# Moving one pattern matmul of each head pair and spreading the finishing of two batches over four pairs, in an attention and mixture-of-experts kernel on one Trainium2 core

## The chip, the core and the metric

The kernel runs on one core of one Trainium2 chip. The metric is the device time of one execution in microseconds (us). The engines are named as in the profile: PE is TensorE (matmuls and transposes; PEld its weight loads), DVE is VectorE, ACT is ScalarE, POOL is GpSimd, SP is SyncE. L305 is line 305 of the kernel before.

## The reference, cut to what matters

Four batches, eight heads, 768 tokens, head size 64. Every query and key falls into one of 64 buckets by the signs of six projections, and a query sees the keys of its own bucket only. The attention's result is then routed token by token to one of eight experts.

```python
q_bits = (einsum('bhsd,dk->bhsk', q, proj) > 0)      # keys likewise
mask = q_bucket[:, :, :, None] == k_bucket[:, :, None, :]
scores = where(mask, q @ k.T / 8, -1e9)
attn = softmax(scores) @ v                           # (4, 8, 768, 64)
x = attn.transpose(0, 2, 1, 3).reshape(3072, 512)
logits = x @ w_gate + modality_bias[modality_id]     # (3072, 8)
e_idx = argmax(logits); gate_w = softmax(logits)[e_idx]
out = gate_w * (relu(x @ w1[e_idx]) @ w2[e_idx])     # w1 512x1024, w2 1024x512
```

## The kernel before

Heads are worked on in 16 pairs, four pairs to a batch: pair `i` belongs to batch `i // 4`. One turn of the outer loop over `i` computes the scores of pair `i`, and prepares later pairs beside it: row maxima (`maxp`) of pair `i + 1`, transposes, signs and patterns (`turn`, `signs`, `patterns`) of pair `i + 2`, and the splitting of the loads (`split`) of pair `i + 3`. Each of these is a Python generator that yields after each piece of work.

The order of PE's instructions is written by hand (`manual_schedule`). Each turn has six strings, `PLAN[0]` to `PLAN[5]`, called string 0 to string 5 here, and each letter takes one piece from one generator. The order of the instructions on the other engines is made by a scheduler, which keeps the data's dependencies and starts what is ready; it lets an instruction that first writes a tile wait until the tile that had the buffer before has been read for the last time.

The letters that matter here:
- `S` one of three score pieces of a string (L305, L306), whose result ACT puts through the exponential (L318, L323); `A` the weighing of the values (L341).
- `M` a row-maximum piece: a matmul (L239 or L245), whose result DVE reduces (L241, L247). `B` is `maxp_back`: PE transposes the negated maxima (L268), and DVE reads the result with three instructions (L270, L270, L271).
- `T` the next of the transposes (L180), signs (L207, read by DVE L209) and patterns (L222, read by L223 and L224) of pair `i + 2`. These are twelve pieces; the strings hold eleven `T`, and `P` takes the twelfth, the last pattern of the second head, in the next turn's string 0.
- `Q` is `sums(i - 1)`: eight matmuls (L359) whose result DVE copies into a new tile `gs` (L362, first pair of a batch) or adds to it (L364).
- `F`, `f`, `E`, `e` take one piece of `finish(b)`, in the four pairs after batch `b`. Its 19 pieces in order: 1 and 2 matmuls for the logits (L374); 3 and 4 their six transposes (L383), read by DVE L384; 5 three transposes of the batch's `gs` (L390), read by L391; 6 L400; 7 L402 to L404; 8 L408; 9 L411; 10 to 13 the routing (`route`: L591 to L597, L600 to L604, small matmuls L609 and L611 with L614 to L617, L620 to L628); 14 to 19 six scatters by POOL into a table in memory (L631).
- `x`, `y` take the pieces of `finish_x` (transposes L422), which writes a batch's attention result to memory, in the third and fourth pair.

Everything that PE writes outside the scores, the maxima and the weighing goes through one pool of two PSUM buffers, `ps_x` (tile `psx`): `T`, `P`, `B`, `Q`, the vector sums `V`, the finishing's matmuls and transposes, and `x`. The maxima have two buffers of their own (`psm`), the scores two (`pss`). The tile `gs` is in a pool with one buffer:

```python
bp = ctx.enter_context(tc.tile_pool(name="bp", bufs=1))
...
        if c == 0:
            gsum[b] = bp.tile([P, HALF], F32, name="gs")
...
        gs = gsum[b]     # in finish(b), piece 5
```

After the 16 pairs the expert stage runs, from about 535 us on; the change does not touch it.

Of the kernel before, what the change touches and what calls it, by code (L numbers as in the profile page):

```python
# [27 lines left out]

LAG = 2
PLAN = (  # L30
    "LvSPMTMSASfMTMfexy",
    "SMTVMSASfMTMey",
    "SMTMSAQFlSMTMEfxy",
    "SMSATWSBMEe",
    "SWMSATFSMTMfWExe",
    "SMTSATSBFfFfWe",
)
FIRST = "mtmtmtmtmtmtmtmbmssnTnbssTnTnTnTnTnTnbTnTTTbT"


# [29 lines left out]
def chain(*gens):  # L70
    for g in gens:
        yield from g


def attention(ctx, actx, tc, a, x_d, l_d, route=None, setup=None):
    nc = tc.nc
    q, k, v, proj = a["q"], a["k"], a["v"], a["proj"]
    NPR = a.get("npair", NP)
# [75 lines left out]
    def split(i, heads=(0, 1)):  # L154

        t = st[i]
        t["n2"] = t.get("n2", {})
        for h in heads:
            qk = t["qk"][h]
            n = nat.tile([P, 2, NT, P], F32R, name="n2")  # L160
            (nc.vector.tensor_copy if i == 0 and h in CFG['rv'] else nc.scalar.copy)(out=n[:, 0, :, 0:64], in_=qk[:, 0])
            nc.scalar.copy(out=n[:, 1, :, 64:128], in_=qk[:, 1])  # L162
            yield
            for x in range(2):
                e = (CFG["rs"] if i == 0 else "PPPP" if i in CFG["rq"] else CFG["sub"])[2 * h + x]
                (nc.vector if e == "D" else nc.gpsimd).tensor_tensor(  # L166
                    out=n[:, x, :, 64 - 64 * x:128 - 64 * x], in0=qk[:, x], in1=n[:, x, :, 64 * x:64 + 64 * x].bitcast(F32), op=ALU.subtract)
            t["n2"][h] = n
            yield

    def turn(i, heads=(0, 1)):

        t = st[i]
        t.update(gens[(i + 2) % 3])
        for h in heads:
            for g in range(3):
                tp = ps_x.tile([P, MAIN], F32, name="psx")
                for j in range(4):
                    x, tt = divmod(4 * g + j, NT)
                    nc.tensor.transpose(tp.bitcast(F32R)[:, j * P:(j + 1) * P], t["n2"][h][:, x, tt], identr)  # L180
                for x in range(2):
                    lo, hi = max(4 * g, NT * x), min(4 * g + 4, NT * x + NT)
                    if lo < hi:
                        (nc.vector.tensor_copy if i == 0 and g == 1 and h in CFG['rv'] else nc.scalar.copy)(
                            out=(t["m2"], t["s2"])[x][h][:, (lo - NT * x) * P:(hi - NT * x) * P], in_=tp[:, (lo - 4 * g) * P:(hi - 4 * g) * P])
                if i == 0 and h == 0:
                    if g == 1:
                        nc.vector.tensor_copy(out=t["m1"][h][QK[h]], in_=t["m2"][h][0:64].bitcast(F32))
                    if g == 2:
                        nc.vector.tensor_copy(out=t["s1"][h][QK[h]], in_=t["s2"][h][64:128].bitcast(F32))  # L190
                else:
                    if g == 1:
                        nc.sync.dma_start(out=t["m1"][h][QK[h]].bitcast(F32), in_=t["m2"][h][0:64].bitcast(F32))
                    if g == 2:
                        nc.sync.dma_start(out=t["s1"][h][QK[h]].bitcast(F32), in_=t["s2"][h][64:128].bitcast(F32))
                yield

    def signs(i, heads=(0, 1)):

        t = st[i]  # L200
        bt = bits[(i + heads[0]) % 2]
        rows = slice(64 * heads[0], 64 * heads[-1] + 64)
        for half in range(2):
            hs = slice(half * HALF, (half + 1) * HALF)
            z = ps_x.tile([P, MAIN], F32, name="psx")
            for o in range(2 * heads[0], 2 * heads[-1] + 2):
                nc.tensor.matmul(z[32 * o:32 * o + 32, 0:HALF], zst, (t["m2"], t["s2"])[o % 2][o // 2][:, hs].bitcast(F32),  # L207
                                 start=True, stop=True, tile_position=(0, 32 * o))
            nc.vector.tensor_scalar(out=bt[rows, hs], in0=z[rows, 0:HALF], scalar1=0.0, scalar2=0.5, op0=ALU.is_gt, op1=ALU.subtract)  # L209
            yield  # L210

    def patterns(i, heads=(0, 1), before=()):

        for _ in before:
            yield
        t = st[i]
        bt = bits[(i + heads[0]) % 2]
        for half in range(2):
            hs = slice(half * HALF, (half + 1) * HALF)
            for h in heads:  # L220
                pp = ps_x.tile([P, MAIN], F32, name="psx")
                nc.tensor.matmul(pp[:, 0:HALF], pat[:, h], bt[:, hs], start=True, stop=True)  # L222
                (nc.vector.tensor_copy if (half if i > 1 else i + h == 0) else nc.scalar.copy)(out=t["m1"][h][PT[h], hs], in_=pp[0:64, 0:HALF])  # L223
                nc.scalar.activation(t["s1"][h][PT[h], hs], pp[64:128, 0:HALF], AF.Relu)  # L224
                yield
# [203 lines left out]
    def first():  # L429

        late = []
        for g in (split(0, (0,)), turn(0, (0,)), split(0, (1,)), signs(0, (0,)), patterns(0, (0,))):
            for _ in g:
                pass
        g = {"m": maxp(0, late, (0,)), "t": chain(turn(0, (1,)), signs(0, (1,)), patterns(0, (1,))),
             "n": maxp(0, late, (1,)), "s": split(1), "T": chain(turn(1), signs(1), patterns(1))}
        for c in FIRST:
            if c == "b":
# [6 lines left out]
    with tc.manual_schedule(engines={mybir.EngineType.PE}):  # L445
        load(1)
        load_v(0)
        load(2)
        first()
        wg = sm.tile([P, 4, 8], F32, name="wg", bufs=1)  # L450
        nc.sync.dma_start(out=wg, in_=a["moe_w_gate"].rearrange("(c p) e -> p c e", p=P))
        gst = fconst.tile([P, 4, 32], F32, name="gst")
        nc.gpsimd.memset(gst, 0.0)
        nc.gpsimd.tensor_copy(out=gst[0:64, :, 0:8], in_=wg[0:64])
        nc.gpsimd.tensor_copy(out=gst[64:128, :, 16:24], in_=wg[64:128])
        ones = fconst.tile([P, 4, 32], F32, name="ones")
        nc.gpsimd.memset(ones, 0.0)
        for c in range(4):
            nc.gpsimd.memset(ones[:, c, c:c + 1], 1.0)
        if setup is not None:  # L460
            setup()
        avs = weigh()
        fins = xs = ts = iter(())
        for i in range(NPR):
            late = []
            ss = score(i)
            ms = maxp(i + 1, late) if i + 1 < NPR else iter(())
            last, ts = ts, chain(turn(i + 2), signs(i + 2), patterns(i + 2)) if i + 2 < NPR else iter(())
            ws = split(i + 3) if i + 3 < NPR else iter(())
            if i % 4 == 0 and i > 0:  # L470
                fins = finish(i // 4 - 1)
            for kt in range(NT):
                for c in PLAN[kt]:
                    if c == "S":
                        next(ss)
                    elif c == "M":
                        next(ms, None)
                    elif c == "T":
                        next(ts, None)
                    elif c == "P":  # L480
                        next(last, None)
                    elif c == "W":
                        next(ws, None)
                    elif c == "A":
                        if i > 0 or kt >= LAG:
                            next(avs)
                    elif c == "B":
                        if late:
                            late.pop(0)()
                    elif c == "v":  # L490
                        vadds(i)
                    elif c == "V":
                        vsums(i)
                    elif c == "Q":
                        if i > 0:
                            sums(i - 1)
                    elif c == "L":
                        if i + 3 < NPR:
                            load(i + 3)
                    elif c == "l":  # L500
                        if i + 1 < NPR:
                            load_v(i + 1)
                    elif c == "F" and i % 4 == 0 or c == "f" and i % 4 == 1:
                        next(fins, None)
                    elif c == "e" and i % 4 >= 2 or c == "E" and i == NPR - 2:
                        next(fins, None)
                    elif c == "x" and i % 4 == 2 or c == "y" and i % 4 == 3:
                        if c == "x" and kt == 0 and i > 4:
                            xs = finish_x(i // 4 - 1, 0, NT)
                        next(xs, None)  # L510
                        next(xs, None)
        for _ in avs:
            pass
        sums(NPR - 1)
# [4 lines left out]
E = 8  # L519
# [463 lines left out]
```

## Time and profile before

| what | value |
|---|---|
| median of three executions | 880.5 us (880.32, 880.5, 881.27) |
| the profiled execution's own time | 876.6 us |
| its span, first to last instruction | 874.7 us |
| PE busy | 815.4 us, 93% |
| DVE, ACT, POOL busy | 584.8, 506.2, 457.1 us |
| mean granted TensorE clock | 0.985 |
| start of pair 1, of pair 15 | 62.7 us, 507.7 us |

A group of instructions in the profile is one line, engine and operation. "Idle before" is the time an engine did nothing before an instruction; the name behind the arrow is what ended that wait. A pair's turn is measured from its first score matmul to the next pair's.

### The profile page before, as it was taken

The page shows a single profiled execution, that of the slowest core. Times are in us where ns is not written, and L with a number is a line of the kernel's source. Part 1 is how long each engine was busy: PE and PEld are TensorE (multiplying, and loading weights), DVE is VectorE, ACT ScalarE, POOL GpSimd, SP SyncE. Part 2 cuts the span into 40 slices and gives each one's busy share as a digit, 9 for nine tenths or more (in the row PEclk, how much of TensorE's full clock was granted, in tenths as well). Part 3 has the DMA queues.
Part 4 walks back from the last instruction along what each step waited for, and adds up shares of the span by engine and source line. Part 5 has one row for each costly group of instructions (what it writes and reads, how often), then busy time and mean ns, then how long its engine had stood idle before and what let it go on. Part 6 is the DMA issues. An engine that isn't in the chain of part 4 may idle for free.

```text
span 874.7 us, 14543 instructions
## 1 busy us (share of the span) xinstructions
PE 815.4 (93%) x5154; PEld 579.8 (66%) x5154; DVE 584.8 (67%) x1029; ACT 506.2 (58%) x953; POOL 457.1 (52%) x347
## 2 busy tenths in 40 slices
PE   5899999998999998999998898879999999999993
PEld 3555655654665554665554555779999999998993
DVE  7776676678677678667776876955555555667550
ACT  5666766665666565566664364444555555557551
POOL 5387678757688757687756687322222221123010
PEclk9899999999999999999999999999999999999997
DMA  6423212221332321340210163796777776677750
GB/s 178 115 60 91 64 41 77 74 54 55 98 85 72 91 60 32 97 118 22 55 46 9 31 229 120 166 266 196 230 231 218 222 227 215 209 240 267 229 155 22
DMA packets 76753, 110.87 MB, mean 127 GB/s; under 512 B 10495, under 2 KB 52095, under 8 KB 76672
## 3 DMA queue, kind: packets, MB, share of 16 engines
q1 hardware_dynamic: 70880, 95.14, 37.6%
q0 software_dynamic: 4928, 13.14, 4.0%
q10 hardware_dynamic: 864, 1.57, 0.9%
q8 instruction: 43, 0.70, 0.4%
q14 instruction: 38, 0.31, 0.1%
HBM read 84.83 MB, written 13.33 MB: 112 GB/s over the span
## 4 chain that ended last, share of the span: by engine, by line
PE 77%; DVE 10%; ACT 4%; DMA 3%; issue 3%; POOL 2%; SPq 0%; POOLq 0%; ACTq 0%; DVEq 0%
PE psu L341 14%; PE pss L305 8%; PE pss L306 6%; PE psm L239 5%; PE yps L835 5%; PE yps L837 5%; PE yps L836 5%; PE hps L795 4%; PE hps L794 4%; PE hps L793 4%; PE psx L207 3%; PE psx L180 3%; PE psm L245 3%; PE psx L222 2%; DVE mx L241 1%
## 5 line engine op out<-in xcount | busy, mean ns | idle before, releaser
L326 POOL TENSOR_TENSOR sp<-sp,pb 128x768 f32<-128x768 f32 x124 | 225.3, 1841 | 42.0 <-ACT pb L323 40.6
L758 DVE TENSOR_TENSOR w<-raw,w 128x1024 fp32r<-128x1024 f32 x108 | 134.9, 1250 | 94.4 <-ACT w L756 93.3
L756 ACT CAST w<-raw 128x1024 fp32r<-128x1024 f32 x112 | 117.2, 1047 | 63.2 <-PE yps L837 55.9
L341 PE MATMUL psu<-pb,vt 128*64 128x512 f32 (+1 forms) x768 | 147.0, 505 | 0.0
L241 DVE TENSOR_REDUCE mx<-psm 128x1 f32<-128x512 f32 x192 | 127.6, 685 | 23.1 <-PE psm L239 22.4
L318 ACT ACTIVATE pb<-pss 128x512 f32<-128x512 f32 x192 | 114.9, 599 | 42.3 <-PE pss L306 22.8
L323 ACT ACTIVATE pb<-pss 128x512 f32<-128x512 f32 x96 | 57.5, 599 | 125.7 <-PE pss L306 122.8
L793 PE MATMUL hps<-xh,w 128*128 128x256 f32 x384 | 108.9, 284 | 2.4 <-DVE hl L800 2.4
L794 PE MATMUL hps<-xl,w 128*128 128x256 f32 x384 | 108.9, 284 | 0.0
L795 PE MATMUL hps<-xh,w 128*128 128x256 f32 x384 | 108.5, 283 | 0.0
L341 PEld LDWEIGHTS psu<-pb,vt 128*64 128x64 f32 x768 | 47.2, 137 | 88.4 <-issue 88.2
L770 POOL DMA_INDIRECT xg<-x_d,tb x26 | 30.8, 1184 | 125.9 <-DMA tb<-tab 87.7
L843 POOL DMA_INDIRECT out<-y,tb x26 | 34.0, 1309 | 118.0 <-ACT y L842 61.3
L835 PE MATMUL yps<-w,hl 128*128 128x512 f32 x208 | 83.6, 402 | 1.9 <-DVE hl L823 1.9
L837 PE MATMUL yps<-w,hh 128*128 128x512 f32 x208 | 81.8, 393 | 0.0
L836 PE MATMUL yps<-w,hh 128*128 128x512 f32 x208 | 81.7, 393 | 0.0
L247 DVE TENSOR_REDUCE mx<-psm 128x2 f32<-128x512 f32 x96 | 66.1, 689 | 22.7 <-PE psm L245 21.5
L305 PE MATMUL pss<-m_0g,s_0g 128*128 128x512 f32 x192 | 78.2, 407 | 0.0
L793 PEld LDWEIGHTS hps<-xh,w 128*128 128x128 f32 x384 | 73.4, 192 | 3.7 <-DVE hl L800 3.0
L166 POOL TENSOR_TENSOR n<-qk,n 128x384 fp32r<-128x384 f32 x36 | 39.7, 1109 | 67.3 <-ACT n L162 60.0
L794 PEld LDWEIGHTS hps<-xl,w 128*128 128x128 f32 x384 | 73.6, 192 | 1.7 <-issue 1.2
L795 PEld LDWEIGHTS hps<-xh,w 128*128 128x128 f32 x384 | 73.5, 192 | 0.0
(214 smaller groups left out, 1763.0 us busy)
## 6 DMA issues: line engine op xcount, KB each, us to landing
raw<-moe_w SPq DMA_DIRECT2D x112, 512.0 KB
qk<-q SPq DMA_DIRECT2D x32, 192.0 KB
qk<-k SPq DMA_DIRECT2D x32, 192.0 KB
vt<-v SPq DMA_DIRECT2D x16, 384.0 KB
x_d<-xs SPq DMA_DIRECT2D x18, 256.0 KB
m_1g<-m_1g SPq DMA_DIRECT2D x16, 192.0 KB
s_1g<-s_1g SPq DMA_DIRECT2D x16, 192.0 KB
m_0g<-m_0g SPq DMA_DIRECT2D x15, 192.0 KB
```

What stands on the lines that cost most here:

```text
L241: nc.vector.tensor_reduce(out=mx[:, qt + j, hi, 0:1], in_=mp, axis=AX.X, op=ALU.max)
L305: nc.tensor.matmul(out, t["s1"][h][:, ks], t["m1"][h][:, cs], start=True, stop=False)
L326: (nc.vector if h and i in CFG["spd"] else nc.gpsimd).tensor_tensor(out=t["sp"][:, h], in0=(t["pb"][0] if kt == 1 else t["sp"])[:, h], in1 ...
L341: nc.tensor.matmul(t["u"][part][64 * h:64 * h + 64, 0:w], t["v"][:, h, kt], t["pb"][kt][:, h, COLS[part]], start=False, stop=(kt == NT - 1 ...
L756: nc.scalar.copy(out=hi, in_=r)
L758: (nc.gpsimd if pool else nc.vector).tensor_tensor(out=lo, in0=r, in1=hi.bitcast(F32), op=ALU.subtract)
L793: nc.tensor.matmul(hps, lo[:, c, fs], xh[:, c], start=(c == 0), stop=False)
L794: nc.tensor.matmul(hps, hi[:, c, fs], xl[:, c], start=False, stop=False)
L795: nc.tensor.matmul(hps, hi[:, c, fs], xh[:, c], start=False, stop=(c == 3))
L835: nc.tensor.matmul(yps[g], hl[fc][:, gs], hi[:, fb], start=(fc == 0), stop=False)
L836: nc.tensor.matmul(yps[g], hh[fc][:, gs], lo[:, fb], start=False, stop=False)
L837: nc.tensor.matmul(yps[g], hh[fc][:, gs], hi[:, fb], start=False, stop=(fc == 7))
```

## The change

The letter `P` moves behind the first `M` of string 0. A table `FIN` says which letters take a piece of `finish`: for pairs below 12 (the finishing of batches 0 and 1) the new letters `G`, `g`, `h`, `k`, one letter for each of the four pairs; for pairs 12 to 15 the old letters, at the places where they were. The function `finish` and all others are as before.

```diff
 PLAN = (
-    "LvSPMTMSASfMTMfexy",
-    "SMTVMSASfMTMey",
-    "SMTMSAQFlSMTMEfxy",
-    "SMSATWSBMEe",
-    "SWMSATFSMTMfWExe",
-    "SMTSATSBFfFfWe",
+    "LvSMPTMSASfMTMfexyhk",
+    "SMTVMSASgfMTMeyhk",
+    "SMTMSAQFGlSMTMEfxyhk",
+    "SMSATGWSBggMEhek",
+    "SWMSATFSMTGMgfWExhek",
+    "SMTSATSBFfFfgWek",
 )
+FIN = (("G", "g", "h", "k"), ("F", "f", "eE", "e"))
...
-                    elif c == "F" and i % 4 == 0 or c == "f" and i % 4 == 1:
-                        next(fins, None)
-                    elif c == "e" and i % 4 >= 2 or c == "E" and i == NPR - 2:
+                    elif c in FIN[i >= NPR - 4][i % 4]:
                         next(fins, None)
```

Counted out for batch 0, whose finishing lies in pairs 4 to 7 (batch 1: the same in pairs 8 to 11):

| pair | before: string (pieces) | after: string (pieces) |
|---|---|---|
| 4 | 2 (1), 4 (2), 5 (3, 4) | 2 (1), 3 (2), 4 (3) |
| 5 | 0 (5, 6), 1 (7), 2 (8), 4 (9), 5 (10, 11) | 1 (4), 3 (5, 6), 4 (7), 5 (8) |
| 6 | 0 (12), 1 (13), 3 (14), 4 (15), 5 (16) | 0 (9), 1 (10), 2 (11), 3 (12), 4 (13) |
| 7 | 0 (17), 1 (18), 3 (19) | 0 to 5 (14 to 19) |

## Rows read from the trace of the kernel before

**Rows 1.** The page's first part: busy time, share of the span and number of instructions of each engine.

```profile
PE 815.4 (93%) x5154; PEld 579.8 (66%) x5154; DVE 584.8 (67%) x1029; ACT 506.2 (58%) x953; POOL 457.1 (52%) x347
```

**Rows 2.** The waits of PE from 60 to 480 us: who waited for whom, us in total, times, longest.

```profile
PE psm L239 <- DVE mx L241: 6.0, 3, 2.0
PE psx L222 <- ACT s_0g L224: 5.5, 10, 0.6
PE psx L383 <- ACT s_0g L224: 3.3, 3, 1.1
```

**Rows 3.** Busy time of the engines in a pair's turn: pairs 4, 5, 6, 7 and 9. Columns: the stretch, its length, then busy time (and instructions) of PE, PEld, DVE, ACT, POOL, granted clock, DMA share, GB/s.

```profile
151.82:184.69 32.87, 31.23 (x206) 18.39 (x206) 22.40 (x41) 21.17 (x44) 23.41 (x17) 1.00 0.22 61
184.69:217.45 32.76, 30.18 (x188) 17.52 (x187) 27.09 (x54) 19.53 (x41) 21.28 (x15) 1.00 0.23 61
217.45:249.21 31.76, 30.95 (x208) 19.10 (x208) 22.11 (x45) 20.05 (x42) 23.68 (x20) 1.00 0.29 74
249.21:280.58 31.37, 30.59 (x197) 18.72 (x196) 22.59 (x39) 20.17 (x42) 26.66 (x18) 1.00 0.34 104
...
313.44:346.22 32.78, 30.18 (x188) 17.50 (x187) 27.24 (x54) 19.55 (x41) 21.29 (x15) 1.00 0.23 61
```

**Rows 4.** The same columns for pair 3, which has no finishing beside it, string by string (0 to 5), and their sum.

```profile
122.12:127.82 5.70, 5.15 (x33) 3.23 (x32) 3.61 (x8) 3.93 (x8) 3.70 (x3) 1.00 0.00 0
127.82:132.76 4.94, 4.94 (x33) 3.25 (x32) 3.69 (x8) 4.72 (x14) 1.02 (x1) 1.00 0.43 93
132.76:138.60 5.84, 5.84 (x42) 3.65 (x41) 3.13 (x6) 2.81 (x8) 5.50 (x5) 1.00 0.48 161
138.60:143.26 4.66, 4.66 (x33) 2.48 (x32) 3.28 (x7) 3.28 (x8) 4.56 (x3) 1.00 0.19 42
143.26:147.96 4.70, 4.70 (x31) 2.47 (x30) 3.93 (x7) 1.83 (x4) 3.96 (x3) 1.00 0.26 84
147.96:151.82 3.86, 3.86 (x23) 2.13 (x22) 2.37 (x5) 3.51 (x8) 3.51 (x2) 1.00 0.00 0
sum 29.70, PE 29.15 PEld 17.21 DVE 20.01 ACT 20.09 POOL 22.25; mean PE 4.86 PEld 2.87 DVE 3.33 ACT 3.35 POOL 3.71
```

**Rows 5.** The same for strings 4 and 5 of pair 4.

```profile
173.79:178.93 5.14, 5.14 (x38) 2.73 (x37) 4.27 (x8) 1.85 (x4) 3.98 (x3) 1.00 0.24 77
178.93:184.68 5.75, 4.66 (x29) 2.79 (x28) 3.75 (x8) 4.61 (x10) 4.65 (x3) 1.00 0.00 0
```

**Rows 6.** The same for strings 0 to 3 of pair 5.

```profile
184.69:190.23 5.54, 5.45 (x36) 3.57 (x35) 3.49 (x7) 2.97 (x6) 2.57 (x2) 1.00 0.00 0
190.23:195.37 5.14, 5.14 (x32) 3.24 (x31) 4.81 (x13) 4.81 (x13) 1.14 (x1) 1.00 0.41 87
195.37:201.95 6.58, 6.10 (x41) 3.64 (x40) 6.33 (x15) 3.12 (x9) 5.89 (x5) 1.00 0.49 143
201.95:208.88 6.93, 4.92 (x32) 2.46 (x31) 6.14 (x12) 3.27 (x8) 4.55 (x3) 1.00 0.13 29
```

**Rows 7.** The timeline around `P` in string 0 of pair 3: start, duration, engine, line, operation, out<-in, shapes, how many in a row; in brackets the idle time before it and what ended it.

```profile
122.83 0.49 ACT L224 ACTIVATE s_0g<-psx 64x384 fp32r<-64x384 f32 x1
...
123.37 0.32 PE L222 MATMUL psx<-bits,pat 128*128 128x384 bf16 x1 [0.55 <-ACT s_0g L224]
...
123.47 0.47 PE L239 MATMUL psm<-s_0g,m_0g 128*128 128x512 f32 x1
...
123.77 0.50 PE L180 MATMUL psx<-identr,n 128*128 128x128 f32 x4
```

**Rows 8.** The timeline of PE at the end of pair 4 and in string 0 of pair 5: the finishing's six transposes and the score matmul behind them, the three transposes of `gs` and the matmul behind them.

```profile
184.06 0.88 PE L383 MATMUL psx<-ident,gsb 128*128 128x128 f32 x6 [1.09 <-ACT s_0g L224]
184.69 0.48 PE L305 MATMUL pss<-m_0g,s_0g 128*128 128x512 f32 x1
...
189.07 0.49 PE L390 MATMUL psx<-ident,gs 128*128 128x128 f32 x3
189.32 0.48 PE L245 MATMUL psm<-s_0g,m_0g 128*128 128x256 f32 x2
```

**Rows 9.** The timeline of PE and DVE around `B` in string 3 of pair 3.

```profile
142.64 0.47 PE L268 MATMUL psx<-identr,nm 128*128 128x128 f32 x4
142.66 0.54 DVE L209 TENSOR_SCALAR bits<-psx 128x384 bf16<-128x384 f32 x1
...
142.95 0.47 PE L239 MATMUL psm<-s_0g,m_0g 128*128 128x512 f32 x1
143.15 0.68 DVE L270 SCALAR_TENSOR_TENSOR m_0g<-psx,m_0g 64x512 fp32r<-64x512 f32 x1
...
144.55 0.69 DVE L271 TENSOR_SCALAR lone<-psx 128x512 fp32r<-128x512 f32 x1
```

**Rows 10.** Two of the finishing's DVE instructions, over all four batches: duration in ns, least, median and most.

```profile
L403 DVE TENSOR_TENSOR rin<-rin,f x4: 193/615/1025, 194.4 to 547.8; 128x48 f32<-128x48 f32 x4
...
L604 DVE TENSOR_TENSOR oh<-rw,rwm x4: 201/944/1633, 202.3 to 553.9; 128x48 bf16<-128x48 f32 x4
```

**Rows 11.** Pair 13, string 3: a wait of PE in the timeline, and the stretch that begins 0.96 us after its end (columns as in rows 3).

```profile
461.31 0.51 PE L239 MATMUL psm<-s_0g,m_0g 128*128 128x512 f32 x1 [1.96 <-DVE mx L241]
...
462.27:465.69 3.42, 3.42 (x17) 0.90 (x16) 0.35 (x2) 1.11 (x2) 0.14 (x1) 0.50 0.00 0
```

## The prediction

> **What bounds the kernel now.** I read the engines' shares first: PE is busy for 93% of the span [rows 1], no other engine reaches 70%. So PE's order sets the end, and a change to it is worth what it takes from PE's idle time or adds to it. Next come PE's waits between 60 and 480 us, the stretch that the change touches [rows 2]. The reader should see that four reasons make up nearly all, and that two of them stand at the letters that are moved: 5.5 us in ten waits at `P` (L222), and 3.3 us in three waits at the finishing's transposes (L383). The 6.0 us at L239 are maxima for which DVE comes late. The third view is the turn of each pair: pair 3, with no finishing, takes 29.70 us [rows 4], pairs 4 and 5 take 32.87 and 32.76 [rows 3]. Pair 9 repeats pair 5 to 0.02 us, so I work out batch 0 and double it. Last come the six strings, since the change moves pieces between strings: pair 4 loses most in string 5 (5.75 against 3.86), pair 5 in string 3 (6.93 against 4.66) [rows 4 to 6].
>
> **P behind the first M.** Nothing is added or removed. In pair 3 `P` waits 0.55 us until 123.37; ACT's L224 ended at 123.32, so a released buffer is used 0.05 us later [rows 7]. That L224 writes the second half of `s1` of the first head, and its reading also frees the buffer that `P` needs. The first `M` multiplies the first head's columns 0 to 511 of the same `s1`, 128 of which L224 has just written. Put first, `M` waits for the same instruction until the same 123.37, and `P` follows it. The two matmuls and the transposes at 123.77 fill the same time in either order. I take 0 for the fourteen `P`. The bounds: a gain of 0.1 us each, the distance from 123.37 to 123.47 that the `M` comes earlier, and a loss of the same for DVE's copy of the pattern, now queued behind the first reduction. What is queued behind it, the third `M`, comes a score piece and a weighing later, which hides it.
>
> **Pair 4.** String 2 keeps its piece. String 3 gains piece 2: its price is 5.14 - 4.70 = 0.44 in string 4 today [rows 4, 5]. It also takes one of the two `psx` buffers between the signs and `B`. In pair 3 the signs' buffer is free at 142.66 + 0.54 + 0.05 = 143.25, and `B` would like to start at 142.64 + 0.44 = 143.08 [rows 9]: 0.17 more. String 4 loses piece 2 and gains piece 3, four of the six transposes that today take 184.69 - 184.06 = 0.63 [rows 8], or 0.42: -0.02. String 5 goes back from 5.75 to 3.86: -1.89, which contains the wait of 1.09. Together -1.30.
>
> **Pair 5, where the wait goes.** String 0: today 5.54, because the 1.09 us before it have covered the wait at `P`, plus three transposes of `gs` (189.32 - 189.07 = 0.25 [rows 8]). Without them it is pair 3's 5.70: +0.16. The wait at `P` is back, now at `M`. String 1: 4.94 + 0.21 for two transposes against 5.14: +0.01. String 2: DVE no longer has the clump of pieces there: 5.84 against 6.58, -0.74.
>
> String 3 decides. `Q` in string 2 of this pair opens a new tile `gs`, of which there is one buffer. Today piece 5 has read the old `gs` in string 0. After the change piece 5 stands in string 3, behind `Q`. So DVE's copy (L362) cannot run until the three transposes have read the old tile, and the sums sit in one of the two `psx` buffers until then. One buffer is left for the signs, `B` and piece 5, in a row. In the times of rows 9: `B` waits for the signs' buffer, 143.25 instead of 142.64, 0.61. DVE starts on it 0.51 later (143.15 - 142.64), at 143.76, and needs 143.15 to 145.24 = 2.09 for its three instructions, so the buffer is free at 145.90. The transposes would have started at 142.95. The hold is 2.95 us. String 3 becomes 4.66 + 0.25 + 2.95 = 7.86 against 6.93: +0.93. The bounds of the hold: 2.4 if DVE reads the signs at once (only 0.05 before `B`), 3.6 if one more instruction of 0.69 stands in DVE's queue ahead. I take 2.95, the row as it is. What else is late: the maxima and scores behind piece 5, whose readers DVE, ACT and POOL gain slack by it.
>
> String 4: pieces 5 to 7 leave DVE with their instructions at once. One of them, L403, took 193 to 1025 ns [rows 10], and behind it stands the reading of the signs (L209), for which the next pattern waits. Nothing to 0.83; I take 0.4, the middle. String 5: piece 8 falls into DVE's idle time there (2.37 busy of 3.86 [rows 4]): 0. Pair 5 together: 0.16 + 0.01 - 0.74 + 0.93 + 0.4 = +0.76.
>
> **Pairs 6 and 7.** Pieces 9 to 11 come over to pair 6, piece 12 moves inside it. In pair 5 today they stand in strings 2 and 3, where DVE is busy (6.33 - 3.13) + (6.14 - 3.28) = 6.06 us longer than in pair 3, and PE is 0.74 + 2.27 = 3.01 longer [rows 4, 6]. Pair 6 has 31.76 - 22.11 = 9.65 us of idle DVE [rows 3], and one piece goes into each string. Bounds 0 and 3.0 (as dense as today); I take 0.5, near the lower end. The scatters: POOL is busy 23.68 + 26.66 - 2 x 22.25 = 5.84 us longer in pairs 6 and 7 than twice pair 3 [rows 3, 4], which I read as the six of them. All now fall into pair 7, 22.25 + 5.84 = 28.1 of its 31.37: they fit, 0; the upper bound is one of them in the way, 5.84 / 6 = 1.0.
>
> **Sum.** -1.30 + 0.76 + 0.5 = -0.04 per batch, -0.1 us for two. The profiled execution takes 876.6 us, 1.9 around its span of 874.7; it would take 876.5. The median of the runs is 880.5, 3.9 above the profiled one; I put the same difference on it: **880.4 us**. No change, then: the waits that the finishing makes today, 1.09 and 2.27 + 0.74 per batch, are paid back by 2.95 at piece 5, the 0.61 of a busier string 3 and the 0.55 at the pair's start.
>
> **The rivals.**
> - *Slower: the clock falls in the hold.* In pair 13 a wait of 1.96 us ended at 461.31, and from 462.27 the granted clock was 0.50, the lower level of 1.2 GHz, for 3.42 us [rows 11]. That string took longer by half of this, 1.7. In pairs 5 and 9 waits of about that size were not followed by a fall: their clock is 1.00 [rows 3]. The hold idles PE for 0.61 and 2.34 us with 0.31 between, more than any of these. If the clock falls in both batches the sum is -0.1 + 3.4, or 883.8; with one it is 882.1. It decides from the first fall on. The Trainium skill (TensorE: Matmul & The Clock Gate, Part 1) says that the throttled state is the default and that only recent activity of PE releases it; the fall in pair 13 agrees, the two waits without one show that a wait of 2 us need not be enough.
> - *Slower: DVE is the clump again, in pair 6.* If piece 11 keeps its worst time (L604, 1633 ns [rows 10]) and the maxima wait as they do today, pair 6 pays 1.6 more: 2 x 1.6, 883.6. Against it: one piece per string. The Trainium skill (GPSIMD Engine Reference, Key points) says that POOL shares its way into SBUF with DVE instructions of two SBUF inputs; the 201 to 1633 ns of one and the same L604 agree. By that rule spreading alone would not shorten these instructions.
> - *Faster: the hold costs less.* If DVE's copy of `gs` or the reading of `B` does not keep PE, strings 3 give back 2.95 per batch: 880.4 - 5.9 = 874.5; with half of it, 877.5. For it: the waits of today do go. Against it: the order of `Q` and piece 5 in the strings.
> - *Faster: P does what its wait suggests.* 0.5 us at each of fourteen, 873.5. Against it: `M` needs the same L224.
>
> **How the numbers follow.** Less than 0.2%, 1.8 us, cannot be told from no change here. The forecast (the wait moves, the clock as before) gets 0.46, with its own range 878 to 883: 0.37 of it within 0.2%, 0.06 faster, 0.03 slower. The clock gets 0.20, DVE in pair 6 0.08, the cheaper hold 0.22, `P` 0.04. So faster 0.06 + 0.22 + 0.04 = 0.32, same 0.37, slower 0.03 + 0.20 + 0.08 = 0.31. The range from 876 to 884 leaves out the free hold (0.10 of the 0.22), `P`, and a clock that falls on top of a DVE clump: about 0.2.
>
> **What the profile after would show.** Right: no wait at L383 at the ends of pairs 4 and 8; a wait of 0.5 us at the first L239 of most pairs instead of L222; in string 3 of pairs 5 and 9 waits of some 0.6 at L268 and 2.3 at L390, both for DVE or ACT readers of `psx`, and L362 behind L390; string 5 of pair 4 at 3.9. Wrong, if L390 does not wait, if pair 5 falls under 31 us, if the granted clock is 0.50 anywhere between 180 and 420 us, or if pair 6 grows by more than 1 us.

## The result: 0.5% slower, where no change was forecast

The changed kernel takes 884.1 us (median of 20 executions) against 879.6 for the kernel before (20 executions beside them): the ratio is 1.0053, with a 95% interval of 1.0034 to 1.0073. The forecast of 880.4 against 880.5 is a ratio of 1.000; the time lies 0.1 us above the top of its range. The executions of the changed kernel spread from 876.5 to 890.4 us (one far outlier left aside), those of the kernel before from 873.9 to 885.3. The profiled execution was the longest of these, 890.4 us, so its stretches are read here with other profiles beside them, not its total.

In the kernel after, line numbers are one higher than before (L240 and L246 are the maxima, L223 the pattern, L269 `B`, L391 piece 5); from L505 on they are one lower. The page's first part, which answers to [rows 1], and PE's waits between 60 and 480 us taken over 60 to 490, which answer to [rows 2]:

```profile
PE 824.7 (93%) x5154; PEld 582.5 (66%) x5154; DVE 586.2 (66%) x1029; ACT 505.7 (57%) x953; POOL 458.2 (52%) x347
```

```profile
PE psm L240 <- ACT s_0g L225: 8.3, 12, 1.3
PE psx L391 <- DVE lone L272: 4.6, 2, 2.3
PE psm L240 <- DVE mx L242: 2.0, 1, 2.0
PE psx L384 <- ACT s_0g L225: 1.1, 1, 1.1
PE psx L269 <- DVE bits L210: 1.1, 2, 0.5
```

The pattern's wait has changed its name and not its size, 5.5 us at L222 before and now in the 8.3 us at L240. Two of the three waits of 1.1 at the finishing's transposes are gone. New are two waits of 2.3 at piece 5 and two of 0.5 at `B`: the hold that the prediction worked out.

The busy time by pair, as in [rows 3] (pairs 4, 5, 6, 7 and 9; the stretch, its length, then PE, PEld, DVE, ACT, POOL, granted clock, DMA share, GB/s):

```profile
153.15:184.74 31.59, 30.94 (x205) 18.25 (x204) 21.63 (x39) 20.07 (x42) 22.34 (x16) 1.00 0.23 64
184.74:219.91 35.17, 31.75 (x190) 18.31 (x189) 23.95 (x47) 20.23 (x42) 22.11 (x15) 0.95 0.21 56
219.91:254.31 34.40, 32.83 (x209) 19.55 (x208) 26.54 (x55) 20.17 (x43) 22.35 (x16) 0.95 0.27 82
254.31:286.73 32.42, 30.92 (x197) 18.74 (x196) 22.09 (x39) 20.05 (x42) 28.07 (x21) 1.00 0.35 86
318.32:353.46 35.14, 31.70 (x190) 18.49 (x189) 23.96 (x47) 20.25 (x42) 22.11 (x15) 0.95 0.21 57
```

Pair 4 gains 1.28 us, as forecast (1.30). Pairs 5, 6 and 7 lose 2.41, 2.64 and 1.05, where 0.76, 0.5 and 0 were forecast. The 1.05 of pair 7 lies in its strings 1 and 2 (6.29 and 6.65 us, 5.70 and 6.29 before). In pairs 5, 6 and 9 the granted clock is 0.95: each holds one stretch of 3.41 us at 0.50, that is 1.2 GHz. The stretches of pairs 5 and 6, with the columns as above:

```profile
210.13:213.54 3.41, 3.41 (x12) 1.42 (x12) 2.95 (x11) 1.19 (x2) 0.13 (x1) 0.50 0.00 0
223.78:227.20 3.42, 3.42 (x11) 1.25 (x11) 1.83 (x6) 1.14 (x3) 1.28 (x1) 0.50 0.00 0
```

The first begins 0.97 us after PE's wait for piece 5 ends (209.16), the second 1.91 us after a wait of 1.27 at the start of pair 6 (221.87). The timeline of string 3 of pair 5, which answers to [rows 8, 9] (start, duration, engine, line, operation; in brackets the idle time and what ended it):

```profile
205.68 0.54 DVE L210 TENSOR_SCALAR bits<-psx 128x384 bf16<-128x384 f32 x1
...
206.37 0.52 PE L269 MATMUL psx<-identr,nm 128*128 128x128 f32 x4 [0.53 <-DVE bits L210]
206.92 0.68 DVE L271 SCALAR_TENSOR_TENSOR m_0g<-psx,m_0g 64x512 fp32r<-64x512 f32 x1 [0.70 <-PE psx L269]
...
208.33 0.69 DVE L272 TENSOR_SCALAR lone<-psx 128x512 fp32r<-128x512 f32 x1
209.16 0.52 PE L391 MATMUL psx<-ident,gs 128*128 128x128 f32 x3 [2.28 <-DVE lone L272]
209.72 0.56 DVE L363 COPY gs<-psx 128x384 f32<-128x384 f32 x1 [0.70 <-PE psx L391]
```

The reader should see the chain in this order: signs read, `B` written, `B` read to its end, piece 5 written, and only then the copy of the sums into `gs`. One buffer serves all of it.

### The profile page after: what moved, and what is told of

Its sections match the earlier page's. It is cut to its first block, busy times and chain, and to the rows that moved or that the text cites. A ratio compares the mean times of both kernels' runs of the same rounds, so it can differ in the third digit from the quotient of the medians.

```text
span 888.6 us, 14545 instructions
## 1 busy us (share of the span) xinstructions
PE 824.7 (93%) x5154; PEld 582.5 (66%) x5154; DVE 586.2 (66%) x1029; ACT 505.7 (57%) x953; POOL 458.2 (52%) x347
## 4 chain that ended last, share of the span: by engine, by line
PE 73%; DVE 9%; DMA 5%; ACT 4%; issue 3%; POOL 2%; SPq 0%; POOLq 0%; ACTq 0%; DVEq 0%
PE psu L342 13%; PE pss L306 7%; PE pss L307 6%; PE psm L240 5%; PE yps L834 5%; PE yps L836 5%; PE yps L835 5%; PE hps L794 4%; PE hps L793 4%; PE hps L792 4%; PE psx L181 3%; PE psx L208 3%; PE psm L246 2%; DMA raw<-moe_w 2%; POOL sp L327 1%
## 5 line engine op out<-in xcount | busy, mean ns | idle before, releaser
L327 POOL TENSOR_TENSOR sp<-sp,pb 128x768 f32<-128x768 f32 x124 | 225.7, 1843 | 52.4 <-ACT pb L324 50.9
L342 PE MATMUL psu<-pb,vt 128*64 128x512 f32 (+1 forms) x768 | 150.8, 516 | 0.0
L769 POOL DMA_INDIRECT xg<-x_d,tb x26 | 33.2, 1279 | 126.4 <-DMA tb<-tab 99.9
L167 POOL TENSOR_TENSOR n<-qk,n 128x384 fp32r<-128x384 f32 x36 | 40.2, 1123 | 66.2 <-ACT n L163 57.4
```

The source lines that it names most:

```text
L327: (nc.vector if h and i in CFG["spd"] else nc.gpsimd).tensor_tensor(out=t["sp"][:, h], in0=(t["pb"][0] if kt == 1 else t["sp"])[:, h], in1 ...
L342: nc.tensor.matmul(t["u"][part][64 * h:64 * h + 64, 0:w], t["v"][:, h, kt], t["pb"][kt][:, h, COLS[part]], start=False, stop=(kt == NT - 1 ...
```

## The experiments

The first four kernels ran on one chip, the next four on a second and the last four on a third, each set with executions of the kernel before beside it; the ratios are against those. The lengths of the strings come from the profiles.

**One half of the change at a time: `P` alone.** The finishing stands as before.

```diff
-    "LvSPMTMSASfMTMfexy",
+    "LvSMPTMSASfMTMfexy",
```

> The kernel before with P alone moved behind the first M. My theory (the first M waits for the same ACT result that P waited for): within 0.1% of before, and the 0.55 us waits stand at the first row-maximum matmul of a pair instead of at the pattern matmul. Rival A (the moved P is what made the changed kernel slower): about 1.005 of before. Rival B (P gives its wait back): 0.992.

Measured: 880.0 us against 877.3, ratio 1.0023 (1.0001 to 1.0045). String 0 grows from 5.70 to 5.76 us in most pairs. In this profile the clock falls in string 3 of pairs 5, 9 and 13 (8.51, 8.50 and 8.46 us, against 6.93, 6.93 and 8.53 before), behind waits that the kernel before has as well. The wait moves as in my theory, and the loss is a little above its 0.1%: the moved letter gains nothing and may lose 0.06 us each time.

**The finishing alone**, with `P` where it was.

```diff
-    "LvSMPTMSASfMTMfexyhk",
+    "LvSPMTMSASfMTMfexyhk",
```

> The spread finishing alone, P at its old place. My theory: all of the change's loss is here, 1.005 of before (about +4.5 us), with PE waits of 0.5 and 2.3 us in string 3 of pairs 5 and 9 and falls of the granted clock behind them. Rival A (P made it slower): 1.000.

Measured: 892.7 us, ratio 1.0157 (1.0128 to 1.0187). The loss belongs to the finishing, and it is three times that of the whole change in the first runs. Strings 2 of pairs 7 and 11 show why: 12.53 and 13.54 us instead of 6.29. The waits of PE between 60 and 490 us:

```profile
PE psm L246 <- DVE mx L242: 8.6, 2, 4.4
```

Such a wait does not stand in the first profile after, and none of my rivals had one in pair 7. The next two runs show it too.

**Two buffers for `gs`**, so that the sums need not wait for piece 5. A small zero tile shares another tile's memory to make room.

```diff
-            gsum[b] = bp.tile([P, HALF], F32, name="gs")
+            gsum[b] = bp.tile([P, HALF], F32, name="gs", bufs=2)
...
-            zt = tmp.tile([P, DM // P], F32, name="zt")
-            nc.gpsimd.memset(zt, 0.0)
+            nc.gpsimd.memset(run[0], 0.0)
+            zt = run[0][:, 0:DM // P]
```

> The changed kernel with two buffers for the tile gs (32 bytes of a start-up tile are saved to make room), so that the copy of the sums need not wait for piece 5. My theory (the hold of the psx buffer and the fall of the clock behind it cost 2.8 + 1.6 us per batch): 8 to 9 us faster than the changed kernel, about 0.995 of before; no waits at L269 and L391 in string 3 of pairs 5 and 9, no fall of the clock there. Rival C (DVE's and ACT's new order in pairs 6 and 7 is the loss, the hold only replaces the old waits): less than 4 us faster than the changed kernel, 1.001 or more of before.

Measured: 892.4 us, ratio 1.0153 (1.0122 to 1.0184). String 3 of pair 5 falls from 8.14 to 5.28 us: the one buffer of `gs` makes the hold. The time, though, missed my 0.995 by far and is that of the rival, since string 5 goes from 3.89 to 5.71, and string 0 of pair 6 is 8.17, with a fall of the clock in it. Strings 2 of pairs 7 and 11 stay at 13.45 and 13.38. PE's waits:

```profile
PE psm L246 <- DVE mx L242: 8.3, 2, 4.3
PE psx L269 <- ACT nm L259: 3.3, 2, 1.7
```

**PE kept busy in the hold.** 36 small matmuls that nothing needs fill the wait behind `B` in pairs 5 and 9. They overwrite part of the weighing of these pairs, so the experts' inputs are other ones.

```diff
             # letter "B"
+            if kt == 3 and i in (5, 9):
+                for _ in range(36):
+                    nc.tensor.matmul(st[i]["u"][1][:, REST:REST + P], pat[:, 0], pat[:, 0],
+                                     start=True, stop=True, skip_group_check=True)
```

> The changed kernel with 36 matmuls of 128 columns, whose result nothing reads, between B and the next g in string 3 of pairs 5 and 9: PE works through the 2.3 us in which it would wait for the buffer. The wait's length stays, its idleness goes. My theory (the granted clock falls because PE idles in the hold): no fall of the clock in string 4 of pairs 5 and 9, 3 us faster than the changed kernel, about 1.002 of before. Rival D (the clock is no part of the loss): the same as the changed kernel, 1.005, or slower by what the 36 matmuls take beyond the wait.

Measured: 890.8 us, ratio 1.0147 (1.0116 to 1.0179). Strings 3 and 4 of pair 5 (columns as above):

```profile
205.50:213.62 8.12, 7.33 (x74) 4.94 (x78) 6.37 (x15) 1.97 (x4) 5.80 (x4) 1.00 0.17 50
213.62:218.33 4.71, 4.71 (x28) 2.44 (x30) 4.47 (x10) 3.07 (x7) 2.42 (x2) 1.00 0.00 0
```

String 3 is as long as with the wait, and the clock stays at 1.00 in both batches; string 4 is 4.71 instead of 6.26. So the hold costs its time whether PE idles or not, and what string 4 pays in the changed kernel is the clock. That the filling kept the clock up is not shown: with the split on POOL, further down, it stays at 1.00 behind the same hold without any filling. The time missed my 1.002, as strings 2 of pairs 7 and 11 again have 12.41 and 12.10.

**The changed kernel once more**, on a second chip, to see whether it too has the new wait.

> The changed kernel once more, beside the next three. If the loss in string 2 of pairs 7 and 11 (PE waits 4 us for a maximum while one DVE subtraction of the split takes 6.5 us, as in the three kernels with the spread finishing) belongs to the changed kernel, 1.015 of before and that wait in the profile; if it depends on a small shift in time, 1.005 and either picture.

Measured: 891.4 us against 877.9, ratio 1.0170 (1.0143 to 1.0197); six executions between 889.9 and 894.8. It has it. Pairs 6 and 7, then string 2 of pair 7, then the first half of the fall inside it, which lasts 6.83 us:

```profile
220.72:253.53 32.81, 31.24 (x209) 19.06 (x208) 26.52 (x55) 20.18 (x43) 22.36 (x16) 1.00 0.29 86
253.53:292.21 38.68, 33.61 (x197) 19.96 (x196) 28.82 (x39) 20.26 (x42) 28.01 (x21) 0.91 0.34 72
```

```profile
265.43:278.90 13.47, 9.18 (x47) 5.41 (x46) 8.72 (x9) 2.92 (x7) 5.98 (x7) 0.75 0.42 94
269.38:272.79 3.41, 2.35 (x9) 2.16 (x10) 3.27 (x6) 0.65 (x2) 1.51 (x3) 0.50 0.58 193
```

In pair 7, DVE's 39 instructions take 28.82 us, where the first profile has 22.09 for the same 39. The timeline of POOL, then of DVE and PE, names the one that is longer:

```profile
260.16 0.96 POOL L630 DMA_INDIRECT tab<-rec,posi  x1 [0.31 <-issue]
261.14 3.63 POOL L327 TENSOR_TENSOR sp<-sp,pb 128x768 f32<-128x768 f32 x2
264.73 1.00 POOL L167 TENSOR_TENSOR n<-qk,n 128x384 fp32r<-128x384 f32 x1
265.69 3.55 POOL L327 TENSOR_TENSOR sp<-pb,pb 128x768 f32<-128x768 f32 x2
```

```profile
263.08 6.58 DVE L167 TENSOR_TENSOR n<-qk,n 128x384 fp32r<-128x384 f32 x1
269.69 1.29 DVE L242 TENSOR_REDUCE mx<-psm 128x1 f32<-128x512 f32 x2
```

```profile
270.44 0.79 PE L246 MATMUL psm<-s_0g,m_0g 128*128 128x256 f32 x2 [4.29 <-DVE mx L242]
```

Piece 12 comes three strings later than before, so the six scatters (L630) begin only at the start of pair 7 and follow each other with pauses of 0.3 us. POOL's sums of the exponentials (L327) pile up behind them, and from 261.14 to 269.24 POOL works without a gap. DVE's part of `split` (L167, both inputs in SBUF) begins in that run at 263.08 and ends at 269.66, 0.42 us after it. Over the whole execution the same instruction has a median of 1.08 us and a least of 0.55. Behind it on DVE stands the reduction of the maxima, whose buffer PE needs: PE waits 4.29 us from 266.15 on, and 3.23 us into this wait, at 269.38, the clock falls.

In the first profile POOL's own subtraction waits for ACT, POOL rests 0.64 us just where DVE's split has begun, and DVE takes 0.80. What shifted ACT there is not shown. The falls in pairs 5 and 6 are not enough for it: in the profile with two `gs` buffers the clock falls in pairs 6 and 10, and both splits behind are long.

```profile
266.15 1.02 POOL L167 TENSOR_TENSOR n<-qk,n 128x384 fp32r<-128x384 f32 x1 [0.64 <-ACT n L163]
...
265.14 0.80 DVE L167 TENSOR_TENSOR n<-qk,n 128x384 fp32r<-128x384 f32 x1
```

**The split taken off DVE.** `rq` lists the pairs whose four subtractions of `split` POOL does alone. Those of pairs 10 and 14 are done in the turns of pairs 7 and 11.

```diff
-    rq=(1, 2)
+    rq=(1, 2, 10, 14)
```

> The changed kernel with DVE's two split subtractions of pairs 10 and 14 (which run in the turns of pairs 7 and 11) given to POOL, so that no DVE instruction with two SBUF inputs stands there beside POOL's additions. Theory E (the scatters, all in string 0 and 1 of pairs 7 and 11 now, push POOL's additions together, and DVE's subtraction gets through only when POOL rests): no wait of 4 us in string 2 of pairs 7 and 11, each about 6 us shorter than in the kernels that show it; about 1.002 of before, what the hold and the falls of the clock cost. Rival F (PE waits there for something else, or POOL itself is late): the wait stays, or moves to a score matmul, 1.012 or more.

Measured: 876.1 us against 877.9, ratio 0.9977 (0.9955 to 0.9999): 15.3 us less than the changed kernel beside it. By the profiles pairs 7 and 11 give back 7.17 and 6.42 us of it, and two missing falls in pairs 5 and 9 another 3.0, together 16.6; the two profiles differ elsewhere too. Its pairs 4 to 7, with no fall and no long split, are the schedule's own price:

```profile
153.09:184.66 31.57, 30.90 (x204) 18.20 (x204) 21.64 (x39) 20.07 (x42) 22.33 (x16) 1.00 0.23 64
184.66:218.26 33.60, 30.16 (x190) 17.71 (x189) 23.97 (x47) 20.25 (x42) 22.11 (x15) 1.00 0.21 59
218.26:251.10 32.84, 31.28 (x209) 19.05 (x208) 26.54 (x55) 20.17 (x43) 22.36 (x16) 1.00 0.29 86
251.10:282.61 31.51, 30.73 (x198) 18.72 (x196) 20.35 (x37) 20.15 (x42) 29.27 (x23) 1.00 0.39 89
```

Against [rows 3]: -1.30, +0.84, +1.08, +0.14, together +0.76 us per batch.

**Both remedies: two `gs` buffers and the split on POOL** (the two diffs above).

> The same, with two buffers for gs. Theory: the hold is gone too, 3 us per batch less than the kernel without the second buffer, as far as the clock does not fall elsewhere: 0.995 to 0.998 of before. If the hold had covered another wait, the same time as that kernel.

Measured: 878.4 us, ratio 1.0007 (0.9983 to 1.0031): not the gain that I expected. The hold is gone (5.29), but string 5 is 5.73 and string 0 of pair 6 is 9.10, with a fall of 6.83 us at 216.45. The sums and piece 5 no longer wait, so the pieces behind them (L404) reach DVE earlier and stand ahead of the maxima that `B` of string 5 needs:

```profile
213.19 1.28 DVE L404 TENSOR_TENSOR rin<-rin,f 128x48 f32<-128x48 f32 x1
```

```profile
215.49 0.41 ACT L259 ACTIVATE nm<-m 128x256 fp32r<-128x256 f32 x1 [1.75 <-DVE m L256]
215.96 0.37 PE L269 MATMUL psx<-identr,nm 128*128 128x128 f32 x2 [1.67 <-ACT nm L259]
```

Pair 5 is 32.61 and pair 6 34.69: the hold had also kept the finishing out of DVE's way.

**Piece 5 ahead of `Q`**, in string 1, and the split on POOL: the old `gs` is read before the new one is opened.

```diff
-    "SMTVMSASgfMTMeyhk",
+    "SMTVMSASgfMTMgeyhk",
...
-    "SMSATGWSBggMEhek",
+    "SMSATGWSBgMEhek",
```

> The changed kernel with the two split subtractions on POOL, and with piece 5 put back ahead of Q by letters alone (piece 5 at the end of string 1 of pairs 5 and 9). Theory: no hold; DVE's pieces 6 to 11 start two strings earlier and may delay the maxima of strings 2 and 3 as before the change (0.5 and 2 us). Between 0.995 and 1.000 of before.

Measured: 874.7 us, ratio 0.9976 (0.9950 to 1.0002), the lowest median of all. String 3 of pair 5 is 5.70; strings 4 and 5 are 6.39 and 5.00, because the maxima are late. Pair 5 takes 34.24 and pair 6 31.92: 66.16 for both, against 66.44 in the kernel with the hold. PE's waits:

```profile
PE psm L240 <- DVE mx L242: 5.9, 5, 2.0
```

**The control: the kernel before with the split on POOL** (the same one-line edit).

> The kernel before with the same two pairs of split subtractions on POOL: the control. Theory E (the subtraction costs nothing there while the scatters run in pair 6): within 0.2% of before. Rival (POOL is the better place anyway, and that is the gain of the kernels with it): 0.997 of before.

Measured: 877.8 us against 877.2, ratio 1.0005 (0.9980 to 1.0030); pair 7 is 31.39. Where DVE isn't held, taking the split from it brings nothing, so what the edit repairs is made by the changed schedule.

**The scatters back in pair 6.** Pieces 9 to 12 stand in string 0 of pair 6 and piece 13 in string 1, all else as in the changed kernel, and the split stays on DVE.

```diff
-    "LvSMPTMSASfMTMfexyhk",
+    "LvSMPTMSASfMTMfehhhhxyk",
...
-    "SMTMSAQFGlSMTMEfxyhk",
-    "SMSATGWSBggMEhek",
-    "SWMSATFSMTGMgfWExhek",
+    "SMTMSAQFGlSMTMEfxyk",
+    "SMSATGWSBggMEek",
+    "SWMSATFSMTGMgfWExek",
```

> The changed kernel with pieces 9 to 12 in string 0 of pairs 6 and 10 and piece 13 in string 1, as before the change; the splits stay on DVE. Only piece 12 has work for PE, so this moves piece 12 from string 3 to string 0, and with it the six scatters from the start of pair 7 back into pair 6. Theory E (the scatters at the start of pair 7 push POOL's additions together): the 6.5 us subtraction and the 4 us wait in string 2 of pairs 7 and 11 are gone, 12 to 15 us faster than the changed kernel, 0.998 to 1.003 of before. Rival G (the wait there comes from elsewhere): 1.015 as the changed kernel.

Measured: 878.9 us against 877.2, ratio 1.0009 (0.9980 to 1.0037). The first and the last scatter on POOL, and string 2 of pair 7:

```profile
230.15 1.17 POOL L630 DMA_INDIRECT tab<-rec,posi  x1 [0.17 <-issue]
...
242.00 0.98 POOL L630 DMA_INDIRECT tab<-rec,posi  x1 [0.17 <-issue]
```

```profile
262.10:268.40 6.30, 6.30 (x47) 4.16 (x45) 3.65 (x7) 2.82 (x8) 5.52 (x6) 1.00 0.55 187
```

DVE's longest split in pair 7 is 2.07 us, as in the kernel before (2.06), and the hold is still there (8.12). So the long split goes with the scatters' place; the small instructions of piece 12 moved with them and were not tested alone. Pair 6 pays 7.89 for its string 0.

**`P` back, the split on POOL.**

```diff
-    "LvSMPTMSASfMTMfexyhk",
+    "LvSPMTMSASfMTMfexyhk",
...
-    rq=(1, 2)
+    rq=(1, 2, 10, 14)
```

> The spread finishing with P at its old place and the split subtractions on POOL, to be held against the same with P moved (0.9977 in its own session). Theory (P is worth nothing): 0.997 to 0.999 of before. Rival A (the moved P costs 0.2%, as its own run hinted): 0.995 to 0.996.

Measured: 883.0 us against 877.2, ratio 1.0054 (1.0021 to 1.0087). Both expectations missed. In this profile the clock falls in pair 5, string 2 of pair 7 is 7.09 instead of 6.29, and string 1 of pair 11 is 7.73 instead of 5.70. The moved `P` is not the loss; that this kernel is slower than the one with both (0.9977 on another chip) I can't explain from one profile.

**The third batch spread as well**, on the kernel with piece 5 ahead and the split on POOL.

```diff
-FIN = (("G", "g", "h", "k"), ("F", "f", "eE", "e"))
+FIN = (("G", "g", "h", "k"), ("G", "g", "h", "k"))
```

> An attempt at a faster one: the spread finishing with piece 5 ahead of Q and the splits on POOL (0.9976 in its session), with the new letters for the third batch too, in pairs 12 to 15. Theory: the waits of 1.1, 2.0 and 1.7 us in pairs 12, 13 and 14 go, and the falls of the clock behind the last two: 3 to 6 us less than without, 0.992 to 0.995 of before. Rival (the third batch's table is late for the expert stage, or its scatters meet the additions of pair 15): no gain, 0.998 or more.

Measured: 886.6 us, ratio 1.0101 (1.0067 to 1.0135). Pairs 12 to 14 become 31.57, 31.40 and 29.11 us (32.85, 33.86 and 31.90 before), as the theory has it, but pair 15 gets a string 3 of 13.39 instead of 3.24, with a fall of the clock of 10.24 us from 524.37 on. PE's waits from 490 to 545 us:

```profile
PE pss L306 <- ACT pb L324: 8.3, 3, 7.7
```

The scores wait for ACT; what keeps ACT there I did not take apart. Pairs 7 and 11 are long again, at 32.42 and 34.92 us with strings 1 of 6.27 and 9.15. That is the picture of the first profile after (32.42 and 34.97, 6.29 and 9.18), here with the split on POOL. So this loss is not the long split.

## Why the prediction was wrong, step by step

**`P` at nothing: nearly right.** The wait went to the first `M` (12 waits, 8.3 us), as worked out. String 0 is 0.06 us longer in each pair with it, inside the bound of 0.1; over fourteen that is 0.8 us that the sum lacked.

**Pair 4: right,** -1.30 forecast, -1.30 measured without a fall, and nearly so string by string (string 3 is 5.40, from 4.66 + 0.44 + 0.17 = 5.27; string 5 is 3.65, from 3.86). That the sum agrees to 0.01 is luck.

**Pair 5: right in sum, with errors that cancel.** +0.76 forecast, +0.84 measured. The hold was forecast as 0.61 + 2.34 = 2.95, and is 0.53 + 2.28 = 2.81. String 3 still grew by 1.19 rather than 0.93: what was left out there, 0.4 us beside the hold, is by luck as much as the 0.4 that I put on string 4. That one did not grow at all (4.69), since L404, 192 to 209 ns in the first profile after, isn't slow there. String 0 is 5.83 where 5.70 was forecast.

**Pair 6: mis-sized,** 0.5 against 1.08. I split the pieces by letters, one into each string. But only pieces 1 to 5 and 12 have work for PE, and only these are held by a letter; the others start as soon as their inputs are ready. So pieces 6 to 11 run straight behind piece 5, from 211.37 on, and pieces 10 and 11 lie across the start of pair 6, where the addition L590, beside an addition of POOL from 218.18 to 220.00, takes 1.42 us (0.21 before):

```profile
218.65 1.42 DVE L590 TENSOR_TENSOR l<-lg,bias 128x48 f32<-128x48 f32 x1
...
220.34 0.21 DVE L594 TENSOR_TENSOR rd<-l,rm 128x48 f32<-128x48 f32 x1
220.58 0.24 ACT L596 ACTIVATE rex<-rd 128x48 f32<-128x48 f32 x1 [0.95 <-DVE rd L594]
220.73 0.58 ACT L324 ACTIVATE pb<-pss 128x512 f32<-128x512 f32 x1
221.33 0.49 ACT L225 ACTIVATE s_0g<-psx 64x384 fp32r<-64x384 f32 x1
221.87 0.50 PE L240 MATMUL psm<-s_0g,m_0g 128*128 128x512 f32 x1 [1.27 <-ACT s_0g L225]
```

ACT's exponential of the routing (L596) waits 0.95 us for DVE, and the pattern's copy (L225) that PE needs stands behind it: PE waits 1.27 us where pair 3 waits 0.55 [rows 7]. What is queued on ACT was missing from my step. The place of the rival "DVE is the clump again, in pair 6" was right, its price was not reached (1.08 of 1.6 with no fall behind it).

**Pair 7: the step that failed.** I wrote that 28.1 us of POOL's work fit into 31.37, put the term at 0 and its bound at 1.0. The sum of POOL's work is right: 28.07 and 28.01 measured. That POOL has time for it does not mean that its neighbour has. In the second profile DVE's subtraction beside it takes 6.58 us, where the longest of the kernel before takes 2.06, and pairs 7 and 11 lose 7.31 and 6.52 us, six to seven times my upper bound: in pair 7 PE waits 4.29 us, and the clock falls for 6.83. In the first profile the same two pairs lose 1.05 and 3.60 without a long split, mostly in their strings 1. The step also had the scatters' place wrong: in the kernel before all six of batch 0 run in pair 6, from 229.18 to 242.01, with POOL's other work between them; their letters did not hold them. The rule that I quoted (the Trainium skill, GPSIMD Engine Reference, Key points: contention with DVE instructions of two SBUF inputs) fits the long L167, but I applied it to the 201 to 1633 ns of small instructions in pair 6 and not to the pair where I had just filled POOL.

**The clock rival** (chance 0.20) was half right. Falls at the hold occur in some executions and not in others: in pairs 5 and 9 of both profiles of the changed kernel, in one of the two pairs where `P` is back, with or without the split on POOL, and in neither where only the split is on POOL or the scatters are back. That is 6 of 12, so the term that I put at nothing is real. One of 3.41 us costs 1.5 to 1.6 us (strings 3 and 4 of a pair together), by 1.7 forecast. That its 883.8 us lies near the measured median is luck, as far as the clocks tell: the mean granted clock of the changed kernel's first executions has a median of 0.981, and that of the kernel before 0.980, 0.980 and 0.981 on the three chips of the experiments, while one fall of 3.41 us would take off 0.002. For the kernel before beside the first executions no clocks are on record. As far as this goes, the median execution hardly has more falls than the kernel before has.

**What this makes of the total.** The schedule alone costs 0.76 us in the first batch and 0.72 in the second; the falls add up to 1.6 each; the long split adds some 7 each. By its pairs, then, the kernel that has only the first of these should lose 1.5 us. It measured 0.9977, a gain of 1.8: in its profile pair 13 is 1.7 shorter, without the fall that the kernel before has there, and the rest stays open. So without the other two the forecast "no change" holds about as well as these runs can tell. In the first runs, with 884.1, most executions can hardly have had two long splits, since the one profiled with two of them took 891.0, and those run beside it 889.9 and more. Which shift of POOL decides it in an execution, and why the first executions showed fewer, stays open. So does string 1 of pair 11 in the first profile (9.18 us, waits of 0.76 and 1.07 around DVE's L425 and a fall at 397.86). A string 1 of more than 7 us in pair 11 stands in three of the ten profiles with the scatters at the start of pair 7, and in none of the other four. Of the 4.5 us that the median of the first runs lost, 1.5 is the schedule, by the pairs of the kernel with the split on POOL; what makes up the other 3 is not shown.

**The marks I had set.** L391 waits, L384 at the end of pair 4 does not, string 5 of pair 4 is 3.64 (3.9 forecast): right. Clock at 0.50 between 180 and 420 us, and pair 6 longer by more than 1: both of the marks for "wrong" came up.

The best kernels are two of those with the split on POOL, 0.9977 with the hold and 0.9976 with piece 5 ahead of `Q`. Only the first interval excludes 1, by 0.0001.

## What to carry to other kernels

Work moved to a lightly loaded engine should be checked twice, once for whether it fits, and once for what runs beside it: ask which instruction of another engine lies in the stretch that is now without a gap, and what stands behind it. A letter or yield places only what has an order of its own; what the scheduler starts when ready does not spread because the letters do. And a tile with one buffer that is opened again ahead of its last reader holds the buffer of whoever wants to write it.

## What the runs showed of the hardware

DVE's subtraction of two SBUF tiles of 128x384 took 0.55 us at best, 0.80 where POOL paused for 0.64, and 6.58 where POOL worked on without a pause; it ended 0.42 us after POOL's run did. But a POOL without a pause is not enough to make it long. In the same profile, in pair 3, it takes 1.09 and ends 0.42 us after POOL's additions, though POOL goes on at once; POOL's own subtraction then takes 1.33 us instead of 1.00:

```profile
143.76 1.09 DVE L167 TENSOR_TENSOR n<-qk,n 128x384 fp32r<-128x384 f32 x1 [1.39 <-issue]
...
144.39 1.33 POOL L167 TENSOR_TENSOR n<-qk,n 128x384 fp32r<-128x384 f32 x1
```

In the long case the same two POOL lines follow each other at 264.73, and DVE does not get through there. What decides between the two is not shown. The least and the most over the 28 of an execution, before and in the second profile after (ns, least, median, most):

```profile
L166 DVE TENSOR_TENSOR n<-qk,n x28: 547/558/2064, 3.7 to 429.5; 128x384 fp32r<-128x384 f32 x28
```

```profile
L167 DVE TENSOR_TENSOR n<-qk,n x28: 552/1083/6578, 3.7 to 449.8; 128x384 fp32r<-128x384 f32 x28
```

The granted clock fell to 0.50 for 3.41 us behind waits of 2.28, and behind one of 1.27, for 6.83 us in and behind one of 4.29, and stayed at 1.00 behind the same 2.28 in the kernel with the split on POOL. A wait's length alone did not tell it apart here. The Trainium skill (TensorE: Matmul & The Clock Gate, Part 1) has the state at 1.2 GHz as the one that idling brings back; the falls behind these waits agree, and no run here shows what decides in the single case.
